# Layer 1's weight conversion: lower parts and guards offered to GpSimd, first v loads moved to SyncE, block 1 given a wider lead

## The chip, the cores and the metric

One core of one Trainium2 chip. The metric is the device time of one execution in microseconds; several runs are timed and the median counts.

## The reference

Three stages, one after the other. Linear attention on q, k, v of shape (8, 8, 576, 64) makes x of shape (4608, 512). Layer 1 takes `elu(x @ w_in) @ w_out` with 2048 hidden columns; layer 2 does the same with other weights and a rational function P(h)/Q(h) in place of elu.

```python
q_s = softmax(q, axis=-1)
k_s = softmax(k, axis=2)
kv = einsum('bhsd,bhse->bhde', k_s, v)
x = einsum('bhsd,bhde->bhse', q_s, kv)      # laid out as (4608, 512)
h = x @ moe_w_in
x = where(h > 0, h, exp(min(h, 0)) - 1) @ moe_w_out
h = x @ moe2_w_in
out = (P(h) / (Q(h) + 1e-6)) @ moe2_w_out
```

All four weight matrices arrive as 64-bit floats; q, k, v are 32-bit floats.

## The kernel before, in words

The tokens are cut into nine blocks of 512, the hidden columns into sixteen slices of 128. A tile is one layer, one block, one slice: an "in" product into one PSUM bank, the activation, and an "out" product that adds into four PSUM banks. Every operand is split into a higher part and a lower part (`copy_hi`, `sub_lo`), and each product is three matmuls: high by high, high by low, low by high. So each half of a tile is 12 matmuls of 128 by 512. The in products stand at lines 785 to 787, the out products at line 827.

Layer 1 starts while attention is still going on. The list `tiles` gives the order: block 0 with its first four slices, block 1 with its first eight, then block 0's other twelve, block 1's other eight, and after that block by block. Until then x of block 0 needs the attention of batch 0 (pairs 0 to 3, two heads each), and x of block 1 that of batch 1 (pairs 4 to 7).

A weight pair of layer 1 (`plan_w1`, line 342; eight pairs of slices, w_in and w_out, 16 loads of 1 MB) goes through these steps, each on a tile of 128 by 1024:

- SyncE loads the 64-bit words into `bits`.
- `floor` (line 321 to 323) raises the top 16 bits of each word to a lower limit, so that a tiny number cannot go wrong in the next step. It is on VectorE.
- `scale` (line 331, ScalarE) makes x from the upper 32 bits, `low` (line 327, VectorE) shifts the lower 32 bits, `join` (line 335, VectorE) puts the two together.
- `hi` (line 299, ScalarE) rounds to the higher part, and `lo` (line 302, VectorE) takes the difference.

The weights of layer 2 go through the same `plan_f32` on tiles of half that size, but `joined` is given there; for layer 1 it is None.

The order of the instructions on each engine comes from a planner in the kernel, class `Plan`. Every step is an operation with a list of engines and a cost on each. Matmuls of layers are "main" operations and get due times from 20 us on; every other operation without a rank of its own gets its due time from what follows it, less its costs and less `lead`. `run` then takes, again and again, the operation and engine that can start earliest by the planner's clock, and the lower due time where two can start at once. VectorE's cost is raised by a quarter of the time that it shares with GpSimd, GpSimd's cost is not raised. What comes out is a fixed order for each engine; on the chip each engine goes through its own list and waits where an input is late.

Three places of this plan matter here. In `plan_f32` the floor is `op(DVE(slow), floor, ...)`, and in `plan_w1` the lower part is `op(DVE(1.4), lo, ...)`. Other lower parts (the activation's, `EITHER`) go to GpSimd at 1.4 or VectorE at 0.8, whichever can start first. In `plan_pair` the four v loads of batch 0 are issued from ScalarE's queue, and the fourth is followed by a small Exp, which loads the activation table:

```python
lv = chain("load_v", ((("ACT" if first else "SP", 0.45),), b["load_v"], (), ...), take=[vkind], dma=0.83)
if n == NP - 1:
    lv["tail"] = 1.5
```

At most eight loads are under way at a time by the plan (`LANES`). Pairs of one batch are spread by `plan.lead`: 3.4 us a pair for batch 0 and 2.0 us a pair for batch 1, the first pair the earliest.

Before 100 us the planner fills gaps of TensorE with matmuls on `ident` (line 276, `keep_warm`), whose results are overwritten.

Two buffers each hold the activation's input `m` and its split output `gs`. The activation of a tile of layer 1 is ScalarE's relu (line 891) and exp (894), VectorE's elu (897), ScalarE's higher part (299), then the lower part (302) on GpSimd or VectorE; only then is `m` free again.

Of the kernel before, what the change touches and what calls it, by code (L numbers as in the profile page):

```python
# [13 lines left out]
AF = mybir.ActivationFunctionType  # L14
# [20 lines left out]
class Plan:  # L35
# [17 lines left out]
    def op(self, engines, fn, after=(), rank=0.0, take=(), free=(), extra=0.0, follow=(), dma=0.0):  # L53
        o = dict(lead=self.lead, rush=0.0, main=False, due=None, follow=[a for a in follow if a is not None], issued=None, engines=engines, fn=fn, after=[a for a in after if a is not None], rank=rank, take=take,
                 free=free, extra=extra, dma=dma, held={}, end=None, next=[], n=len(self.ops))
        waits = o["after"] + o["follow"]
        o["left"] = len(waits)
        for a in waits:
            a["next"].append(o)
        self.ops.append(o)  # L60
        return o
# [120 lines left out]
def linear_attention_elu_rational(  # L182
# [31 lines left out]
    nc = tc.nc  # L214
# [41 lines left out]
    def DVE(c=0.75):  # L256
        return (("DVE", c),)
# [4 lines left out]
    def POOL(c=1.4):  # L262
        return (("POOL", c),)
# [52 lines left out]
    def plan_f32(st_op, st_of, new_x, n, rank, x_kinds, joined=None):  # L316

        b = {}
        fast, slow = whole(n)

        def floor(e):
            top = st_of().rearrange("p n t -> p (n t)").bitcast(I16).rearrange("p (n u) -> p n u", u=4)[:, :, 3]
            nc.vector.tensor_scalar(out=top, in0=top, scalar1=FLOOR, scalar2=None, op0=ALU.max)

        def low(e):
            t = st_of()[:, :, 0]
            nc.vector.tensor_scalar(out=t, in0=t, scalar1=29, scalar2=None, op0=ALU.logical_shift_right)

        def scale(e):
            b["x"] = new_x()  # L330
            nc.scalar.activation(out=b["x"], in_=st_of()[:, :, 1].bitcast(F32), func=AF.Prelu, scale=2.0**-112, alpha=-2.0**32)

        def join(e):
            xi = b["x"].bitcast(I32)
            nc.vector.scalar_tensor_tensor(out=joined().bitcast(I32) if joined else xi, in0=xi, scalar=3, in1=st_of()[:, :, 0], op0=ALU.logical_shift_left,
                                           op1=ALU.bitwise_or)

        o1 = op(DVE(slow), floor, [st_op], rank)
        o2 = b["own"] = op(ACT(0.25 + n * 0.00095), scale, [o1], rank, take=x_kinds)
        o3 = op(DVE(fast), low, [st_op], rank)  # L340
        return op(DVE(slow), join, [o2, o3], rank), b

    def plan_w1(f, which, rank, load_rank, after):

        w = (moe_w_in, moe_w_out)[which]
        kind = f"w{f // 2}_{which}"
        b = {}

        def load(e):
            b["st"] = main.tile([P, 2 * DM, 2], I32, tag=kind, name="bits", bufs=1)  # L350
            nc.sync.dma_start(out=b["st"].rearrange("p n t -> p (n t)"), in_=w[f // 2].bitcast(I32))

        def new_x():
            (name, _), = x["own"]["held"].items()
            return at.tile([P, 2 * DM], F32, tag=name, name="x", bufs=1)

        def pairs(ap):
            return ap.rearrange("p (i n) -> p i n", i=2)

        def hi(e):  # L360
            b["hl"] = new_slots(f, which)
            copy_hi(b["hl"][:, :, 0], pairs(x["x"]))

        def lo(e):
            sub_lo(e, b["hl"][:, :, 1], pairs(x["x"]), b["hl"][:, :, 0])

        b["op"] = op(SP, load, after, load_rank, take=[kind], dma=2.6)
        o, x = plan_f32(b["op"], lambda: b["st"], new_x, 2 * DM, rank, [("x", "st")])
        own = op(ACT(1.05), hi, [o], rank)
        o = op(DVE(1.4), lo, [own], rank, free=[(("x", "st"), x["own"])])  # L370
        at_ops.append(o)
        for i in range(2):
            slot_ready[0, f + i, which], slot_owner[0, f + i, which] = o, b["op"]
        return o
# [57 lines left out]
    def pair_fns(n):  # L432
# [20 lines left out]
        def load_v(e):  # L453
            if j > 1 and b["v_op"]["held"].get("x"):
                vt = at.tile([P, 2 * TB], F32, tag="x", name="vt", bufs=1)
            elif vkind == "xs":
                vt = main.tile([P, 2 * TB], F32, tag="xs", name="vt", bufs=8)[:, 0:NS * (2 * D + 2)]
            else:
                vt = at.tile([P, NS * (2 * D + 2)], F32, tag="vb", name="vb", bufs=1)
            if j > 1:  # L460
                b["vt"] = vt[:, 0:S // D * (D + 1)].rearrange("p (j c) -> p j c", c=D + 1)
                nc.sync.dma_start(out=vt[:, 0:S // D * (D + 1)], in_=v[j, hp, :, 0:S // D * (D + 1)])
                return
            (nc.scalar if e == "ACT" else nc.sync).dma_start(out=vt, in_=v[j, hp])
            if n == NP - 1:
                nc.scalar.activation(out=spare, in_=ident[:, 0:1], func=AF.Exp)
            b["vt"] = vt.rearrange("p (j h c) -> p j h c", j=NS, h=2)

        def load_q(e):
# [188 lines left out]
    def plan_pair(j, hp, r):  # L658
        n = j * NP + hp
        b = pair_fns(n)  # L660
        kkind, vkind, qkind = b["kinds"]
        first = j == 0
        o = plan_q(n, r, None, 0.0)
        b["t_op"] = t1 = chain("q_T", (PE(0.47), b["q_T"], [o], r + 1.5), take=["bank", "qT"], free=[(qkind, b["q_op"])], extra=0.2)
        b["qc"] = chain("q_copy", (ACT(), b["q_copy"], [t1], r + 1.7), free=[("bank", t1)])

        def kT_top(e):
            b["top"] = at.tile([P, 1], F32, tag="top", name="top", bufs=2)
            nc.vector.tensor_reduce(out=b["top"], in_=flat()[:, 0:S], op=ALU.max, axis=AX.X, negate=True)

        def kT_exp(e):
            nc.scalar.activation(out=flat()[:, 0:S], in_=flat()[:, 0:S], func=AF.Exp, bias=b["top"])

        def flat():
            return b["kt"].rearrange("p j n -> p (j n)")

        def k_turn(e):
            b["tp"] = [acc_bank() if first else bank() for _ in range(2)]
            for i in range(NS):
                w = min(P, S - i * P)  # L680
                nc.tensor.transpose(b["tp"][i // 4][0:w, i % 4 * P:(i % 4 + 1) * P], flat()[:, i * P:i * P + w], ident)

        def k_back(e):
            nc.scalar.activation(out=flat()[:, 0:TB], in_=b["tp"][0], func=AF.Copy)

        def k_tail(e):
            dst, src = flat()[0:S - TB, TB:TB + P], b["tp"][1][0:S - TB, 0:P]
            if e == "ACT":
                nc.scalar.activation(out=dst, in_=src, func=AF.Copy)
            else:  # L690
                nc.vector.tensor_scalar(out=dst, in0=src, scalar1=1.0, scalar2=None, op0=ALU.mult)

        l = b["k_op"] = chain("load_k", (SP, b["load_k"], (), r - 3), take=[kkind], dma=0.82)
        lv = chain("load_v", ((("ACT" if first else "SP", 0.45),), b["load_v"], (), r - 2.2 if first else r - 2), take=[vkind],
                   dma=0.83)
        if n == NP - 1:
            lv["tail"] = 1.5
        top = chain("k_top", (DVE(0.72), kT_top, [l], r - 0.5), take=["top"])
        o = chain("k_exp", (ACT(0.7), kT_exp, [top], r - 0.4), free=[("top", top)])
        tp_kind = "acc" if first else "bank"  # L700
        kT = chain("k_turn", (PE(0.6), k_turn, [o], r - 0.3), take=[tp_kind, tp_kind, "kvd"], extra=0.2)
        o1 = chain("k_back", (ACT(), k_back, [kT], r), free=[(tp_kind, kT)])
        o2 = chain("k_tail", ((("ACT", 0.3), ("DVE", 0.25)), k_tail, [kT], r))
        kvm = chain("kv_mm", (PE(0.9), lambda e: b["kv_mm"](e, b["tp"][1]), [o1, o2, lv], r + 0.5), extra=0.2,
                    free=[(kkind, l), (vkind, lv)])
        o = chain("kv_norm", (DVE(0.33), b["kv_norm"], [kvm], r + 0.7))
        kv_ready[n] = chain("kv_div", ((("ACT", 0.31), ("DVE", 0.25)), b["kv_div"], [o], r + 0.7), free=[(tp_kind, kT)])
        kvd_of[n] = kT
        if hp % 2:
            plan_x(n, r, [state[n - 1]["qc"], b["qc"]])  # L710
# [282 lines left out]
        for which in range(2):  # L993
            w1.append(plan_w1(f, which, None, None, [w1[-6]] if len(w1) > 5 else []))
    for hp in range(NP):
        plan.lead = 0.01 + 2.0 * (NP - 1 - hp)
        plan_pair(1, hp, 0.0)
    plan.lead = 0.0
    for n, t in enumerate(tiles[:NB * KF]):
# [72 lines left out]

    with tc.manual_schedule():
        nc.vector.memset(qbias, 2.0**-48 * (1.0 + 1e-6))
        make_identity(nc, ident)

        def load_ab(e):
# [95 lines left out]
```

## Time and profile before

| what | us |
|---|---|
| median of 3 runs | 1592.34 |
| the 3 runs | 1591.29 to 1597.28 |
| the profiled execution | 1595.57 |
| span of that execution, first to last instruction | 1593.8 |
| TensorE busy with matmuls in the span | 1573.5 (99%) |
| VectorE busy | 1041.6 (65%) |
| ScalarE busy | 1040.5 (65%) |
| GpSimd busy | 762.5 (48%) |

The page names TensorE PE, VectorE DVE, ScalarE ACT, GpSimd POOL and SyncE SP. All times within the span count from its first instruction. Busy time of TensorE holds the filling matmuls on `ident`, too, and matmuls overlap in the pipeline, so it is no measure of useful work by itself. An instruction's duration holds what it waits inside its engine, for instance for access to memory; the time before it, in which the engine stood still, is listed apart as idle with what ended it.

### The profile page before, as it was taken

How to read it: one execution, taken by the hardware profiler on the slowest of the kernel's cores; microseconds unless marked ns; L12 is line 12 of the kernel's file. 1: busy time of each engine (PE TensorE's matmuls, PEld its weight loads, DVE VectorE, ACT ScalarE, POOL GpSimd, SP SyncE). 2: the span in 40 equal slices, each digit the busy share in tenths (PEclk: the TensorE clock that was granted, in tenths of full speed). 3: DMA queues.
4: the chain of work that ended last, by engine and by line, in shares of the span. 5: the costliest groups of instructions: out<-in, count | busy, mean ns of one | idle time of the engine just before them, and what ended most of it. 6: DMA issues, size and time to landing. Idle time of an engine off the chain costs nothing.

```text
span 1593.8 us, 22864 instructions
## 1 busy us (share of the span) xinstructions
PE 1573.5 (99%) x8382; PEld 1356.0 (85%) x8382; DVE 1041.6 (65%) x1627; ACT 1040.5 (65%) x1835; POOL 762.5 (48%) x551
## 2 busy tenths in 40 slices
PE   8999999999999999999999999999999999999998
PEld 7787888888888888888887888888888888888886
DVE  8888666554655556431227767686778687777776
ACT  6767655554655455444558767777777777777676
POOL 3333323232332222232657566656666666666554
PEclk9999999999999999999999999999999999999999
DMA  9513443232332322101432010101010000100000
GB/s 352 229 56 103 150 137 114 85 110 97 102 111 88 103 95 92 52 14 37 137 91 80 1 53 1 54 0 54 0 46 8 29 26 21 34 7 21 1 27 27
DMA packets 48784, 113.31 MB, mean 71 GB/s; under 512 B 5664, under 2 KB 5664, under 8 KB 46624
## 3 DMA queue, kind: packets, MB, share of 16 engines
q1 hardware_dynamic: 48096, 110.52, 20.2%
q8 instruction: 66, 1.08, 0.3%
q10 hardware_dynamic: 576, 1.33, 0.2%
q14 instruction: 46, 0.38, 0.1%
HBM read 82.47 MB, written 29.36 MB: 70 GB/s over the span
## 4 chain that ended last, share of the span: by engine, by line
PE 87%; ACT 4%; issue 4%; DVE 3%; POOL 2%; DMA 0%; POOLq 0%; DVEq 0%; ACTq 0%
PE acc L827 43%; PE ps L785 14%; PE ps L787 14%; PE ps L786 14%; POOL gs L302 2%; PE ps L639 1%; PE ps L512 1%; ACT p L930 1%; ACT s L926 1%; ACT m L936 0%; ACT m L939 0%; DVE s L942 0%; DVE m L945 0%; PE acc L276 0%; DMA e<-in_q_dram 0%
## 5 line engine op out<-in xcount | busy, mean ns | idle before, releaser
L785 PE MATMUL ps<-xs,w_in 128*128 128x512 f32 x1152 | 439.7, 382 | 6.6 <-DVE m L897 3.6
L787 PE MATMUL ps<-xs,w_in 128*128 128x512 f32 x1152 | 438.4, 381 | 0.0
L786 PE MATMUL ps<-xs,w_in 128*128 128x512 f32 x1152 | 438.4, 381 | 0.0
L827 PE MATMUL acc<-gs,w_out 128*128 128x512 f32 x1728 | 403.8, 381 | 1.3 <-POOL gs L302 0.8
L827 PEld LDWEIGHTS acc<-gs,w_out 128*128 128x128 f32 x1728 | 324.0, 189 | 52.9 <-ACT gs L299 2.8
L302 POOL TENSOR_TENSOR gs<-m,gs 128x512 fp32r<-128x512 f32 x119 | 163.0, 1370 | 360.4 <-ACT gs L299 332.0
L785 PEld LDWEIGHTS ps<-xs,w_in 128*128 128x128 f32 x1152 | 218.7, 190 | 42.1 <-issue 6.5
L786 PEld LDWEIGHTS ps<-xs,w_in 128*128 128x128 f32 x1152 | 218.7, 190 | 31.3 <-DVE xs L302 0.2
L787 PEld LDWEIGHTS ps<-xs,w_in 128*128 128x128 f32 x1152 | 218.7, 190 | 31.2
L897 DVE SCALAR_TENSOR_TENSOR m<-m,ps 128x512 f32<-128x512 f32 x144 | 98.6, 684 | 206.8 <-ACT m L894 198.1
L302 POOL TENSOR_TENSOR gs<-p,gs 128x512 fp32r<-128x512 f32 x72 | 116.3, 1615 | 235.5 <-issue 196.9
L933 POOL TENSOR_TENSOR s<-s,m 128x512 f32<-128x512 f32 x144 | 218.4, 1517 | 16.9 <-ACT m L922 16.9
L827 PE MATMUL acc<-w_out,gs 128*128 128x512 f32 x864 | 202.4, 381 | 2.6 <-ACT gs L299 1.6
L827 PE MATMUL acc<-w_out,g 128*128 128x512 f32 x864 | 199.8, 379 | 0.5 <-POOL g L302 0.5
L891 ACT ACTIVATE m<-ps 128x512 f32<-128x512 f32 x144 | 85.8, 596 | 166.9 <-PE ps L787 126.8
L942 DVE SCALAR_TENSOR_TENSOR s<-s,m 128x512 f32<-128x512 f32 x144 | 142.6, 990 | 71.7 <-ACT m L939 71.5
L827 PEld LDWEIGHTS acc<-w_out,gs 128*128 128x128 f32 x864 | 162.9, 189 | 29.4 <-POOL gs L302 4.6
L827 PEld LDWEIGHTS acc<-w_out,g 128*128 128x128 f32 x864 | 163.2, 189 | 24.0 <-POOL g L302 0.9
L930 ACT ACTIVATE p<-ps,a_sb 128x512 f32<-128x512 f32 x144 | 112.1, 779 | 80.7 <-POOL gs L302 73.9
L299 ACT ACTIVATE gs<-m 128x512 fp32r<-128x512 f32 x144 | 90.5, 629 | 92.4 <-PE acc L827 78.5
L951 DVE SCALAR_TENSOR_TENSOR p<-p,a_sb,ps 128x512 f32<-128x512 f32 x144 | 107.4, 746 | 56.9 <-ACT m L922 56.8
L955 DVE SCALAR_TENSOR_TENSOR p<-p,a_sb,m 128x512 f32<-128x512 f32 x144 | 136.6, 949 | 2.1
(124 smaller groups left out, 1906.8 us busy)
## 6 DMA issues: line engine op xcount, KB each, us to landing
x<-e SPq DMA_DIRECT2D x36, 256.0 KB, 2.0
e<-x SPq DMA_DIRECT2D x36, 256.0 KB, 3.0
out_dram<-e SPq DMA_DIRECT2D x36, 256.0 KB, 2.0
bits<-in_moe_w_in_dram SPq DMA_DIRECT2D x8, 1024.0 KB, 11.0
bits<-in_moe_w_out_dram SPq DMA_DIRECT2D x8, 1024.0 KB, 11.9
st<-in_moe_w_in_dram SPq DMA_DIRECT2D x16, 512.0 KB, 4.5
w<-st SPq DMA_DIRECT2D x32, 256.0 KB, 2.0
st<-in_moe_w_out_dram SPq DMA_DIRECT2D x16, 512.0 KB, 4.5
```

The lines of the kernel that those rows point to most:

```text
L299: nc.scalar.activation(out=hi, in_=src, func=AF.Copy)
L302: engine[e].tensor_tensor(out=lo, in0=src, in1=hi.bitcast(F32), op=ALU.subtract)
L785: nc.tensor.matmul(o, w[:, 0, kk, :], two(x[:, 0]), start=(kk == 0), stop=False)
L786: nc.tensor.matmul(o, w[:, 0, kk, :], two(x[:, 1]), start=False, stop=False)
L787: nc.tensor.matmul(o, w[:, 1, kk, :], two(x[:, 0]), start=False, stop=(kk == KD - 1))
L827: nc.tensor.matmul(turned(o), lhsT, two(rhs), start=(f == f0 and n == 0), stop=(f == f1 and n == 2))
L897: nc.vector.scalar_tensor_tensor(out=b["m"], in0=b["m"], scalar=-1.0, in1=b["h"], op0=ALU.add, op1=ALU.max)
L930: nc.scalar.activation(out=b["p"], in_=b["h"], func=AF.Identity, scale=a_sb[:, 3:4], bias=a_sb[:, 2:3])
L933: engine[e].tensor_tensor(out=b["s"], in0=b["s"], in1=b["a"], op=ALU.add)
L942: nc.vector.scalar_tensor_tensor(out=b["s"], in0=b["s"], scalar=1.0 + 1e-6, in1=b["a"], op0=ALU.add, op1=ALU.mult)
L951: nc.vector.scalar_tensor_tensor(out=b["p"], in0=b["p"], scalar=a_sb[:, 1:2], in1=b["h"], op0=ALU.add, op1=ALU.mult)
L955: nc.vector.scalar_tensor_tensor(out=b["p"], in0=b["p"], scalar=a_sb[:, 0:1], in1=b["a"], op0=ALU.add, op1=ALU.mult)
```

## The change

Five edits. The lower part of layer 1's weights goes to GpSimd at a planned 2.5 us in place of VectorE at 1.4. Layer 1's floor may go to VectorE at 1.39 or to GpSimd at 0.2 + 1024 * 0.002 = 2.25, whichever can start first. The v loads of batch 0 are issued by SyncE, with the rank of the others. The table is loaded by an Exp on `qbias` as ScalarE's first instruction. The lead of batch 1's pairs goes from 2.0 to 3.0 us a pair.

```diff
         def floor(e):
-            nc.vector.tensor_scalar(out=top, in0=top, scalar1=FLOOR, scalar2=None, op0=ALU.max)
+            engine[e].tensor_scalar(out=top, in0=top, scalar1=FLOOR, scalar2=None, op0=ALU.max)
...
-        o1 = op(DVE(slow), floor, [st_op], rank)
+        o1 = op((("DVE", slow), ("POOL", 0.2 + n * 0.002)) if joined is None else DVE(slow), floor, [st_op], rank)
...
-        o = op(DVE(1.4), lo, [own], rank, free=[(("x", "st"), x["own"])])
+        o = op(POOL(2.5), lo, [own], rank, free=[(("x", "st"), x["own"])])
...
-            (nc.scalar if e == "ACT" else nc.sync).dma_start(out=vt, in_=v[j, hp])
-            if n == NP - 1:
-                nc.scalar.activation(out=spare, in_=ident[:, 0:1], func=AF.Exp)
+            nc.sync.dma_start(out=vt, in_=v[j, hp])
...
-        lv = chain("load_v", ((("ACT" if first else "SP", 0.45),), b["load_v"], (), r - 2.2 if first else r - 2), take=[vkind],
+        lv = chain("load_v", (SP, b["load_v"], (), r - 2), take=[vkind],
                    dma=0.83)
-        if n == NP - 1:
-            lv["tail"] = 1.5
...
     for hp in range(NP):
-        plan.lead = 0.01 + 2.0 * (NP - 1 - hp)
+        plan.lead = 0.01 + 3.0 * (NP - 1 - hp)
         plan_pair(1, hp, 0.0)
...
         nc.vector.memset(qbias, 2.0**-48 * (1.0 + 1e-6))
+        nc.scalar.activation(out=spare, in_=qbias, func=AF.Exp)
         make_identity(nc, ident)
```

## Rows read from the trace of the kernel before

**Rows 1.** Windows: us, then each engine's busy us (instructions), PEclk, DMA share, GB/s.

```profile
0.00:27.30 27.30, 23.60 (x218) 19.84 (x218) 20.07 (x42) 16.78 (x29) 10.76 (x14) 1.00 0.96 375
27.30:65.00 37.70, 35.40 (x279) 28.49 (x277) 36.37 (x54) 28.32 (x49) 16.41 (x11) 1.00 0.60 219
65.00:131.00 66.00, 61.64 (x275) 52.40 (x274) 57.55 (x52) 45.99 (x56) 19.70 (x9) 0.97 0.32 125
200.00:1594.00 1394.00, 1383.89 (x7222) 1196.04 (x7220) 878.98 (x1397) 900.74 (x1595) 686.85 (x495) 1.00 0.17 56
```

**Rows 2.** Timeline of TensorE: start us, us, line, op, [idle before <- what ended it].

```profile
27.30 0.48 PE L785 MATMUL ps<-xs,w_in 128*128 128x512 f32 x1
...
34.68 3.74 PE L276 MATMUL acc<-ident 128*128 128x128 f32 x32
...
39.39 1.78 PE L827 MATMUL acc<-gs,w_out 128*128 128x512 f32 x7 [0.54 <-DVE w_out L302]
...
51.44 0.95 PE L520 MATMUL ps<-vb,kt 128*64 128x65 f32 x20 [1.62 <-ACT kt L689]
```

**Rows 3.** Waits of TensorE: waited for, us in total, times, longest us.

```profile
PE ps L785 <- DVE m L897: 3.6, 2, 2.2
```

**Rows 4.** Chain of work that ended last: start us, us, what; two of its pieces.

```profile
0.73 3.77 DMA e<-in_q_dram
...
25.95 1.04 DVE w_in L302
```

**Rows 5.** Timeline of VectorE, ScalarE and GpSimd, 16 to 40 us, on the first weights.

```profile
16.32 1.27 DVE L323 TENSOR_SCALAR bits<-bits 128x1024 int16<-128x1024 int16 x1
...
23.89 1.06 ACT L299 ACTIVATE w_in<-x 128x1024 fp32r<-128x1024 f32 x1 [0.29 <-DVE x L335]
...
30.30 2.19 DVE L323 TENSOR_SCALAR bits<-bits 128x1024 int16<-128x1024 int16 x1
...
33.84 1.04 ACT L299 ACTIVATE w_out<-x 128x1024 fp32r<-128x1024 f32 x1
...
38.12 1.21 DVE L302 TENSOR_TENSOR w_out<-x,w_out 128x1024 fp32r<-128x1024 f32 x1
```

**Rows 6.** DMA issues: line's tiles, queue, count, KB each, us to landing.

```profile
e<-x SPq DMA_DIRECT2D x36, 256.0 KB, 3.0
```

**Rows 7.** Timeline of VectorE and GpSimd where both work, 95 to 120 us.

```profile
95.94 1.28 POOL L302 TENSOR_TENSOR gs<-m,gs 128x512 fp32r<-128x512 f32 x1 [1.89 <-ACT gs L299]
...
96.05 2.56 DVE L335 SCALAR_TENSOR_TENSOR x<-x,bits 128x1024 int32<-128x1024 int32 x1
...
112.91 3.05 DVE L335 SCALAR_TENSOR_TENSOR x<-x,bits 128x1024 int32<-128x1024 int32 x2
...
113.19 4.98 POOL L302 TENSOR_TENSOR gs<-m,gs 128x512 fp32r<-128x512 f32 x1 [3.56 <-ACT gs L299]
...
115.80 1.40 DVE L323 TENSOR_SCALAR bits<-bits 128x1024 int16<-128x1024 int16 x1
```

**Rows 8.** Instructions on tile bits, 0 to 60 us: duration ns min/median/max, first and last start.

```profile
L327 DVE TENSOR_SCALAR bits<-bits x5: 695/999/1585, 20.4 to 56.0; 128x1024 int32<-128x1024 int32 x5
L335 DVE SCALAR_TENSOR_TENSOR x<-x,bits x5: 1232/1521/2029, 21.9 to 58.4; 128x1024 int32<-128x1024 int32 x5
```

**Rows 9.** Groups of VectorE and GpSimd, 65 to 131 us: count | busy us, mean ns | idle before.

```profile
L335 DVE SCALAR_TENSOR_TENSOR x<-x,bits 128x1024 int32<-128x1024 int32 x10 | 15.9, 1601 | 1.1 <-ACT x L331 0.7
L323 DVE TENSOR_SCALAR bits<-bits 128x1024 int16<-128x1024 int16 x9 | 13.3, 1473 | 0.0
L327 DVE TENSOR_SCALAR bits<-bits 128x1024 int32<-128x1024 int32 x9 | 9.1, 1023 | 0.0
L302 DVE TENSOR_TENSOR w_in<-x,w_in 128x1024 fp32r<-128x1024 f32 x6 | 8.4, 1398 | 0.4 <-ACT w_in L299 0.2
L302 DVE TENSOR_TENSOR w_out<-x,w_out 128x1024 fp32r<-128x1024 f32 x5 | 7.2, 1442 | 0.2 <-ACT w_out L299 0.2
...
L302 POOL TENSOR_TENSOR gs<-m,gs 128x512 fp32r<-128x512 f32 x9 | 19.7, 2189 | 42.1 <-ACT gs L299 42.1
```

## The prediction

> **What bounds the kernel now.** I read the windows by stage first. From 200 us on TensorE is busy 1383.89 of 1394 us [rows 1]; nothing that the change touches acts there, since layer 1's weights are ready by then. So the change is worth what is lost before. In the first 27.3 us TensorE does no product of a layer: the first one starts at 27.30 [rows 2]. Between 27.3 and 65 us it is busy 35.40 of 37.70 us, but the busy time holds a filler of 3.74 us [rows 1, 2]. Between 65 and 131 us it stands still 4.4 us, and its granted clock falls to 0.97 on the mean, that is, part of the stretch ran at the lower of its two levels, 1.2 GHz, after these pauses; 3% of 66 us is 2.0 us [rows 1].
>
> The windows also say who is the limit in these stages: VectorE is busy 36.37 of 37.70 us and then 57.55 of 66 us, GpSimd only 16.41 and 19.70 [rows 1]. The chain of waits runs through VectorE from the first q load to the lower part of the first w_in [rows 4]. So far this speaks for moving work to GpSimd.
>
> The timeline of both engines speaks against it. A join on VectorE, which takes 1.23 us at best, took 2.56 us when it began 0.11 us behind a lower part on GpSimd of 1.28 us: it waited for that one to end [rows 7, 8]. The other way round, a lower part on GpSimd took 4.98 us because two joins and a floor followed one another on VectorE from 112.91 to 117.20 us; it ended at 118.17 [rows 7]. Operations with SBUF inputs on these two engines exclude each other here. Of such work the kernel gets no more done by sharing it out.
>
> **The change part by part.** The sum is made against the profiled execution, 1595.57 us, span 1593.8. That one lies 3.2 us above the median of 1592.34; I take the same difference off the median. A measurement of this kernel can tell about 0.5% from no change, 8 us, so the bounds are 1584.4 and 1600.3.
>
> *Term 1, the start.* The first q load lands 3.77 us after its issue [rows 4]; a load of the same 256 KB alone takes 3.0 [rows 6]. Before, four v loads run beside it from ScalarE's queue; in SyncE's queue they come behind the first q and k. So 0.8 us. The v loads are 4 x 128 x 650 x 4 bytes = 1.33 MB, at the 375 GB/s of this stretch 3.5 us [rows 1], but they stood ahead of the weights before as well, so the weights' loads land no later. Their issues now pass through SyncE ahead of the later q, k and weight loads, and these leave ScalarE; I cost that at nothing, as the DMA share is 0.96 [rows 1] and the transfers cover the issue; without that cover it would be four issues. The table load at once costs nothing either: ScalarE has 16.78 us of work in 27.3 [rows 1], and before the first Exp it waits for data. The floor at 16.32 stood on VectorE for 1.27 us ahead of attention work [rows 5]; on GpSimd it is off that queue, -1.27. The lower part of w_in is not seen on GpSimd at this size: the nearest row is 1.28 us for half the size [rows 7], so 2.56. The high part ends at 24.95 (23.89 + 1.06), so on GpSimd the lower part would end at 27.5, where VectorE ended at 27.0 (25.95 + 1.04) [rows 4, 5]: +0.5. Sum -0.8 - 1.27 + 0.5 = -1.6. Bounds: +0.5 if nothing upstream moves; -0.8 - 2 x 1.27 - 1.21 = -4.5 if all that VectorE is rid of by then counts.
>
> *Term 2, the gap at 35 us.* TensorE fills 3.74 us and then stands 0.54 until VectorE has made the lower part of w_out [rows 2]. Its high part was done at 34.88; VectorE came to it at 38.12, 3.2 us later, and took 1.21 [rows 5]. On GpSimd one other lower part may stand in front (1.4), and it takes 1.35 more. Of the floor at 30.30, 2.19 us [rows 5], I count half as gained upstream, because on GpSimd it holds up VectorE's joins in turn. -3.2 + 1.4 + 1.35 - 1.1 = -1.5. Bounds +1.35 and -4.3 (the whole gap).
>
> The price of a floor on GpSimd is not in the trace. Below: 1.27, as on VectorE; above: 2.56, two inputs of that size. I take 2.1, nearer the upper row because that is GpSimd's own.
> The Trainium skill (GPSIMD Engine Reference, 3.1 Elementwise) gives 1.03 cycles an element for an operation with one input; at its 1.2 GHz I estimate 0.9 us, by which a floor there would be cheaper than on VectorE and term 4 below about 0. No run so far shows it.
>
> *Term 3, block 1's pairs.* The wider lead puts the first pair of batch 1 due 9 us ahead in place of 6, the next 6 in place of 4. The wait of 1.62 us at 51.44 on such a pair's key tail [rows 2] should shrink: -1.0; bounds -1.6, and +2.0 if the pairs now displace the first weights on ScalarE and VectorE by about two operations.
>
> *Term 4, the weights from 65 to 131 us.* At their undisturbed prices the operations that exclude one another need 10 x 1.23 (joins) + 9 x 1.27 (floors) + 9 x 0.70 (lows) + 11 x 1.21 (lower parts) + 9 x 1.28 (activation's lower parts on GpSimd) = 54.8 of 66 us [rows 5, 7, 8, 9]. Eleven lower parts at 2.56 add 14.9, so 69.7: 3.7 us too much; with nine floors at 2.1 on GpSimd another 7.5. Some of it is relieved since the activation's lower parts go to VectorE when GpSimd is taken, and some can slip past 131 us, because the last slices are used last. VectorE's long runs, which held GpSimd for 4.98 us, get rarer: of the 3.6 us waited for VectorE's m [rows 3] I take 2 back, and put 3 of new waiting against it: +1. Bounds -5.6 (3.6 and the 2.0 of the clock) and +15 (14.9 with no relief).
>
> Sum: -1.6 - 1.5 - 1.0 + 1.0 = -3.1. 1592.3 - 3.1 = **1589.2 us**.
>
> **The rivals.** *GpSimd becomes the wait (slower).* Lower parts of 2.56 us, stretched by whatever VectorE holds, stand in GpSimd's queue in front of the activation's; ScalarE's relu then waits for `m`, of which there are two, and behind it in ScalarE's queue the scale and high part of the next weights; TensorE runs out of products. It decides from where the excess of term 4 can no longer slip: then about 14 of the 3.7 + 7.5 us and of the same in 27 to 65 us fall on TensorE, and with terms 1 to 3 at -3 it is +11: 1603. For it: the 4.98 us row [rows 7] and a planner that does not raise GpSimd's cost. Against: GpSimd's idle time, 46 of 66 us [rows 1].
> The Trainium skill says the same as a rule (SBUF — State Buffer, Who interferes with whom): the pair of ports is an exclusive lock, taken by VectorE with two SBUF inputs and by GpSimd for a whole instruction. By that rule the trace agrees for joins and lower parts; for the floor, with one input, the rule asks for a two-port mode, and the row of 2.19 us says that it waits too. The page Perfetto Trace Analysis (Optimizing Scalar/DVE Operations) adds that moving work between these two might not help.
>
> *VectorE alone was the limit (much faster).* GpSimd's holes take the work without collisions: terms at their lower bounds, -4.5 - 4.3 - 1.6 - 5.6 = -16; two thirds of that, -11: 1581. For it: VectorE's 96% and 87%. Against: 54.8 of 66 us are already exclusive work.
>
> *It doesn't do what it says.* The planner has GpSimd free at the wrong moments and leaves floors on VectorE, the start is set by the loads as before, and term 4 eats the little: 1592.
>
> **How the numbers follow.** Forecast (a few us faster) 0.35, slower 0.25, much faster 0.22, nothing 0.18. Of the slower case two thirds lie above 1600.3, of the much faster nearly all below 1584.4, and some of the forecast's spread beyond either. So faster 0.24, same 0.57, slower 0.19. The range, 1580 to 1602, takes in the forecast, the middle of the much faster case and most of the slower one; the bounds of term 4 set its upper end.
>
> **What would show it.** First product at 25.7 rather than 27.30; filler and wait before the first out products under 3 us; lower parts of the weights on GpSimd at 2.6 us where alone and up to 5 beside joins; VectorE's busy share in 27 to 131 us down by some 30 us; waits of TensorE in 65 to 131 us between 3 and 6 us, on GpSimd's lower parts instead of VectorE's m. The forecast is wrong if these waits pass 12 us, or if the first product starts before 23.5 us and the later waits vanish.

## The result, and the profile after

The changed kernel takes 1615.98 us at the median (five runs, 1614.2 to 1619.99), the kernel before 1592.34 beside it. The ratio is 1.015 with a 95% interval of 1.0135 to 1.0164: slower by 23.6 us, where 3.1 us faster was forecast, and outside the range of 1580 to 1602. The profiled execution has a span of 1614.2 us, 20.4 more than before.

The windows of the changed kernel, in the columns of [rows 1]:

```profile
0.00:27.30 27.30, 22.18 (x223) 18.64 (x225) 19.79 (x40) 17.56 (x33) 18.97 (x18) 1.00 0.96 362
27.30:65.00 37.70, 29.75 (x197) 23.26 (x197) 26.94 (x39) 23.49 (x36) 36.36 (x16) 0.91 0.63 242
65.00:131.00 66.00, 51.08 (x224) 41.09 (x217) 52.64 (x43) 35.48 (x50) 60.61 (x17) 0.91 0.24 96
131.00:200.00 69.00, 66.95 (x341) 57.32 (x344) 35.60 (x54) 41.79 (x75) 33.11 (x21) 0.99 0.30 98
200.00:1614.00 1414.00, 1404.26 (x7383) 1213.68 (x7372) 901.48 (x1433) 919.50 (x1644) 695.67 (x502) 1.00 0.17 57
```

The window of the kernel before that [rows 1] leaves out:

```profile
131.00:200.00 69.00, 69.00 (x397) 59.26 (x396) 48.60 (x87) 48.67 (x108) 28.73 (x22) 1.00 0.37 126
```

All of the loss lies where the change acts. From 200 us on TensorE stands still 9.7 us, as before (10.1). Between 27.3 and 131 us it stands 7.95 + 14.92 = 22.9 us; before it was 2.3 + 4.4 = 6.7 [rows 1]. The granted clock is 0.91 in both stretches; 9% of 103.7 us is 9.3 us, against 2.0 before. Together that is 23.5 us more. The filler in this stretch fell from 3.7 us [rows 2] to 1.3, so 2.5 us of the standing have only changed their name, and 2.1 us come after 131 us: 23.1. The span grew by 20.4; this sum is higher in part because it counts the low clock also while TensorE stands. Counted in matmuls, the traces have 576 of the layers' products by 200 us, and 676 before: 100 at 0.22 us each are 22 us.

The third column of busy times has VectorE down from 36.37 to 26.94 and from 57.55 to 52.64. The last one, GpSimd, is up from 16.41 to 36.36 of 37.70 and from 19.70 to 60.61 of 66 us. The limit has moved to GpSimd, which hardly rests. The groups of GpSimd from 27.3 to 131 us say with what (count, then busy us, mean ns and idle time before):

```profile
L323 POOL TENSOR_SCALAR bits<-bits 128x1024 int16<-128x1024 int16 x10 | 52.9, 5352 | 0.0
L302 POOL TENSOR_TENSOR w_in<-x,w_in 128x1024 fp32r<-128x1024 f32 x7 | 18.5, 2637 | 0.1
L302 POOL TENSOR_TENSOR w_out<-x,w_out 128x1024 fp32r<-128x1024 f32 x5 | 15.7, 3140 | 3.5 <-ACT w_out L299 3.5
```

Ten floors take 52.9 us, more than the twelve lower parts beside them (34.2). The view of line 323 (duration in ns: least, median, largest; first and last start) shows that this isn't a matter of collisions alone:

```profile
L323 POOL TENSOR_SCALAR bits<-bits x12: 4312/5352/6228, 16.8 to 115.6; 128x1024 int16<-128x1024 int16 x12
```

The shortest floor on GpSimd takes 4.31 us. The plan has 2.25, and the prediction bounded it by 2.56.

How this reaches TensorE is seen at the first weights, in the timeline of the changed kernel:

```profile
25.88 1.06 ACT L299 ACTIVATE w_in<-x 128x1024 fp32r<-128x1024 f32 x1 [0.89 <-DVE x L335]
...
28.29 4.74 POOL L323 TENSOR_SCALAR bits<-bits 128x1024 int16<-128x1024 int16 x1
...
32.86 2.35 POOL L302 TENSOR_TENSOR w_in<-x,w_in 128x1024 fp32r<-128x1024 f32 x1
...
35.26 0.80 PE L783 MATMUL ps<-xs,w_in 128*128 128x512 f32 x1 [4.68 <-POOL w_in L302]
```

The high part of the first w_in is ready at 26.94. Its lower part on GpSimd begins at 32.86, since the plan had put the floor of a later weight ahead of it, in the belief that it would be over in 2.25 us. TensorE waits 4.68 us for it, and then its clock is at half: in the chain of waits the matmuls that follow stand 0.43 us apart until 40.29, and 0.22 from there.

```profile
36.05 0.43 PE ps L781
...
40.29 0.22 PE ps L782
```

The waits of TensorE between 27 and 131 us (in total, times, longest):

```profile
PE acc L823 <- DVE gs L302: 6.6, 3, 4.5
PE ps L783 <- POOL w_in L302: 4.7, 1, 4.7
PE ps L782 <- DVE xs L302: 4.2, 1, 4.2
PE acc L823 <- ACT gs L299: 4.0, 2, 3.5
PE acc L823 <- POOL gs L302: 2.2, 1, 2.2
```

Most of them name another engine than GpSimd. The rows behind three of the longest show why. For the 3.5 us, ScalarE's higher part came late because in ScalarE's own list a scale stood in front of it, and that waited for a floor.

```profile
115.64 6.23 POOL L323 TENSOR_SCALAR bits<-bits 128x1024 int16<-128x1024 int16 x1
...
121.90 1.13 ACT L331 ACTIVATE x<-bits 128x1024 f32<-128x1024 f32 x1 [7.38 <-POOL bits L323]
...
122.94 0.61 ACT L299 ACTIVATE gs<-m 128x512 fp32r<-128x512 f32 x1
...
123.61 0.48 PE L823 MATMUL acc<-gs,w_out 128*128 128x512 f32 x1 [3.52 <-ACT gs L299]
```

For the 4.5 us, the activation's lower part came late because in VectorE's list a floor and a low stood in front of it, and these took 3.47 and 2.81 us beside two lower parts on GpSimd (the first began at 100.37); the least of each before is 1.27 and 0.70.

```profile
101.27 3.47 DVE L323 TENSOR_SCALAR bits<-bits 128x1024 int16<-128x1024 int16 x1
...
103.50 3.28 POOL L302 TENSOR_TENSOR w_in<-x,w_in 128x1024 fp32r<-128x1024 f32 x1
...
104.52 2.81 DVE L327 TENSOR_SCALAR bits<-bits 128x1024 int32<-128x1024 int32 x1
...
107.25 0.68 DVE L302 TENSOR_TENSOR gs<-m,gs 128x512 fp32r<-128x512 f32 x1
...
107.98 4.33 PE L823 MATMUL acc<-gs,w_out 128*128 128x512 f32 x11 [4.54 <-DVE gs L302]
```

The 4.2 us have the same form with the floors of GpSimd beside: x's lower part on VectorE stood behind a floor of 3.67 us there. So the floors hurt through the lists that wait for them, and floors and lower parts both hurt through stretched operations on VectorE.

### The profile page after: what moved, and what is told of

Its sections match the earlier page's. It is cut to its first block, busy times and chain, and to the rows that moved or that the text cites. A ratio compares the mean times of both kernels' runs of the same rounds, so it can differ in the third digit from the quotient of the medians.

```text
span 1614.2 us, 22798 instructions
## 1 busy us (share of the span) xinstructions
PE 1574.2 (98%) x8342; PEld 1354.0 (84%) x8342; DVE 1036.4 (64%) x1606; ACT 1037.8 (64%) x1836; POOL 844.7 (52%) x571
## 4 chain that ended last, share of the span: by engine, by line
PE 85%; ACT 4%; POOL 4%; DVE 3%; issue 2%; DMA 1%; POOLq 0%; SPq 0%; DVEq 0%; ACTq 0%
PE acc L823 42%; PE ps L781 14%; PE ps L783 14%; PE ps L782 14%; POOL gs L302 1%; POOL bits L323 1%; PE ps L637 1%; PE ps L510 1%; DVE bits L327 1%; ACT p L926 1%; POOL w_in L302 1%; POOL w_out L302 1%; ACT s L922 1%; ACT m L932 0%; DMA st<-in_moe_w_in_dram 0%
## 5 line engine op out<-in xcount | busy, mean ns | idle before, releaser
L823 PE MATMUL acc<-gs,w_out 128*128 128x512 f32 x1728 | 408.8, 384 | 14.9 <-DVE gs L302 6.6
L302 POOL TENSOR_TENSOR gs<-m,gs 128x512 fp32r<-128x512 f32 x110 | 144.4, 1313 | 311.3 <-ACT gs L299 294.9
L299 ACT ACTIVATE gs<-m 128x512 fp32r<-128x512 f32 x144 | 90.3, 627 | 92.6 <-PE acc L823 77.2
```

The source lines that it names most:

```text
L299: nc.scalar.activation(out=hi, in_=src, func=AF.Copy)
L302: engine[e].tensor_tensor(out=lo, in0=src, in1=hi.bitcast(F32), op=ALU.subtract)
L823: nc.tensor.matmul(turned(o), lhsT, two(rhs), start=(f == f0 and n == 0), stop=(f == f1 and n == 2))
```

## The experiments

The theory after the result: floors cost 4.3 us and more on GpSimd, and the lists of all engines wait for them. The rivals: the lower parts and the access that the two engines share; or the loads and the lead. The kernel before ran beside each group of runs at 1593.9 us (1593.84 to 1593.95), and the ratios are to it.

### One part undone, or one part alone

Floors back on VectorE, all else as changed:

```diff
-            engine[e].tensor_scalar(out=top, in0=top, scalar1=FLOOR, scalar2=None, op0=ALU.max)
+            nc.vector.tensor_scalar(out=top, in0=top, scalar1=FLOOR, scalar2=None, op0=ALU.max)
...
-        o1 = op((("DVE", slow), ("POOL", 0.2 + n * 0.002)) if joined is None else DVE(slow), floor, [st_op], rank)
+        o1 = op(DVE(slow), floor, [st_op], rank)
```

> The changed kernel with all floors of layer 1 back on VectorE, all else of the change kept. Theory (the floors' price: 4.31 us on GpSimd where nothing disturbs them, planned at 2.25, twelve of them): most of the 23.6 us go, 1588 to 1596. Rival (the lower parts on GpSimd and the shared access): at most a third goes, 1606 to 1614. Rival (loads and lead): nothing goes, 1612 to 1618.

Measured: 1600.9 us, 1.0044 (1.0027 to 1.006). About 15 us go, which is most of it and more than either rival allowed. But the theory's window ended at 1596, and the time stays 7 us above the kernel before: something else costs as well.

The kernel before with the floors offered and nothing else:

```diff
-            nc.vector.tensor_scalar(out=top, in0=top, scalar1=FLOOR, scalar2=None, op0=ALU.max)
+            engine[e].tensor_scalar(out=top, in0=top, scalar1=FLOOR, scalar2=None, op0=ALU.max)
...
-        o1 = op(DVE(slow), floor, [st_op], rank)
+        o1 = op((("DVE", slow), ("POOL", 0.2 + n * 0.002)) if joined is None else DVE(slow), floor, [st_op], rank)
```

> The kernel before with only the floors offered to GpSimd at the planned 2.25 us. Theory (the floors' price): slower than before by 10 to 25 us, 1602 to 1617, with GpSimd's floors at 4.3 us or more. Rival (the lower parts): within 4 us of before. Rival (loads and lead): within 4 us of before.

Measured: 1613.16 us, 1.0118 (1.0102 to 1.0135), +19.3 us, as the theory had it. All 16 floors go to GpSimd here, at 4.27 us or more:

```profile
L323 POOL TENSOR_SCALAR bits<-bits x16: 4272/4790/5952, 13.9 to 120.0; 128x1024 int16<-128x1024 int16 x16
```

The kernel before with the lower parts on GpSimd and nothing else:

```diff
-        o = op(DVE(1.4), lo, [own], rank, free=[(("x", "st"), x["own"])])
+        o = op(POOL(2.5), lo, [own], rank, free=[(("x", "st"), x["own"])])
```

> The kernel before with only the lower parts of layer 1's weights on GpSimd at the planned 2.5 us. Theory (the floors' price): within 5 us of before, 1588 to 1597, since the lower parts take 2.36 us undisturbed, less than planned. Rival (the lower parts and the shared access): 10 to 20 us slower, 1602 to 1612. Rival (loads and lead): as before.

Measured: 1601.77 us, 1.005 (1.0035 to 1.0065), +7.9 us. The theory had 1597 at most, so it falls short; the rival had 10 us at least, so it is right in kind and too high. The groups of both engines from 65 to 131 us, which answer to [rows 9], show where it comes from:

```profile
L335 DVE SCALAR_TENSOR_TENSOR x<-x,bits 128x1024 int32<-128x1024 int32 x11 | 20.2, 1858 | 1.3 <-ACT x L331 1.3
L327 DVE TENSOR_SCALAR bits<-bits 128x1024 int32<-128x1024 int32 x9 | 18.2, 2024 | 0.0
L323 DVE TENSOR_SCALAR bits<-bits 128x1024 int16<-128x1024 int16 x9 | 17.1, 1899 | 0.0
...
L302 POOL TENSOR_TENSOR w_in<-x,w_in 128x1024 fp32r<-128x1024 f32 x6 | 19.4, 3236 | 0.0
L302 POOL TENSOR_TENSOR w_out<-x,w_out 128x1024 fp32r<-128x1024 f32 x4 | 13.1, 3278 | 4.0 <-ACT w_out L299 4.0
```

The low on VectorE takes 2024 ns on the mean, 1023 before; the floor 1899, 1473 before; the join 1858, 1601 before [rows 9]. VectorE is rid of eleven lower parts (8.4 + 7.2 us), and yet it is busy longer in this stretch, 61.12 us beside 57.55. A join and two of the activation's lower parts are new in it (some 3 us); the rest of what it gave up, 15.6 us, comes back as longer lows, floors and joins. The Trainium skill (Perfetto Trace Analysis, Optimizing Scalar/DVE Operations) says that moving work between these two engines might not help; this run agrees with that sentence.

Loads, table and lead as changed, nothing moved to GpSimd (the edits of the change's diff at `load_v`, `lv`, the Exp on `qbias` and):

```diff
-        plan.lead = 0.01 + 2.0 * (NP - 1 - hp)
+        plan.lead = 0.01 + 3.0 * (NP - 1 - hp)
```

> The kernel before with only the v loads on SyncE, the table at once and the lead of 3.0: no work moved to GpSimd. Theory (the floors' price) and the rival of the lower parts: within 4 us of before, by the prediction's terms 1 and 3 some 1 to 2 us faster, 1588 to 1593. Rival (loads and lead): 10 us slower or more.

Measured: 1592.86 us, 0.9994 (0.9984 to 1.0004), no difference that can be told. The three parts alone give +19.3, +7.9 and -1.0, in sum 26.2; the whole change has 23.6. They nearly add up.

The changed kernel with the lower parts back on VectorE:

```diff
-        o = op(POOL(2.5), lo, [own], rank, free=[(("x", "st"), x["own"])])
+        o = op(DVE(1.4), lo, [own], rank, free=[(("x", "st"), x["own"])])
```

> The changed kernel with the lower parts back on VectorE, floors still offered to GpSimd. If floors and lower parts add up (18 to 19 us and 7 to 8 us alone, loads and lead -1): 1608 to 1613. If lower parts hurt only because floors fill GpSimd, they cost more together than alone: 1602 to 1607.

Measured: 1610.11 us, 1.0104 (1.0088 to 1.012): they add up here, too. This run has the plainest picture of a list held up. Between a query's exponential and its product with the reciprocal sum, the plan of GpSimd has three floors:

```profile
36.58 14.13 POOL L323 TENSOR_SCALAR bits<-bits 128x1024 int16<-128x1024 int16 x3
...
50.54 1.04 POOL L575 TENSOR_TENSOR qt<-qt,mx 128x512 f32<-128x512 f32 x1
...
51.64 1.11 PE L581 MATMUL ps<-ident,qt 128*128 128x128 f32 x4 [7.24 <-POOL qt L575]
```

At the planned price three floors are 6.75 us; they took 14.13, and TensorE stood still for 7.24 us.

### The wrong price, or the work itself

The changed kernel with the floor's price in the plan near the measured one:

```diff
-        o1 = op((("DVE", slow), ("POOL", 0.2 + n * 0.002)) if joined is None else DVE(slow), floor, [st_op], rank)
+        o1 = op((("DVE", slow), ("POOL", 0.2 + n * 0.0041)) if joined is None else DVE(slow), floor, [st_op], rank)
```

> The changed kernel with the planner's price of a floor on GpSimd at 0.2 + 1024 * 0.0041 = 4.4 us in place of 2.25; the plan then has 8 of the 16 floors on GpSimd in place of 12. If the harm was the planner's wrong price (the lists of all engines made for a GpSimd that is twice as fast), the time comes near that without floors there, 1600.9: 1599 to 1605. If the harm is the work itself, at 4.3 us and more each, two thirds of the 15 us stay: 1608 to 1613.

Measured: 1611.24 us, 1.0113 (1.0095 to 1.0131), as the second expectation had it. Knowing the price saves 5 us of 15; the rest stays with the eight floors that the plan still gives to GpSimd. It does so because, by its code, it compares when an operation can begin, not when it ends: an idle GpSimd wins over a VectorE that is free 1 us later and three times as fast.

The floors alone offered at the planned price, but on GpSimd as a 32-bit maximum, which leaves the guard out there (the plan's line as in the run with the floors alone):

```diff
...
+            if e == "POOL":
+                top = st_of()[:, :, 1].bitcast(F32)
+                nc.gpsimd.tensor_scalar(out=top, in0=top, scalar1=-3e38, scalar2=None, op0=ALU.max)
+                return
...
```

> The kernel before with floors offered to GpSimd, but on GpSimd the floor is a maximum of the 32-bit upper halves as floats with -3e38, at the same stride of 8 bytes and count of 1024: it leaves the guard out there. If 16-bit access is what makes 4.3 us: 1.1 to 2.4 us each, and a time of 1588 to 1600. If it is the single-input loop of GpSimd or the stride: still 4 us or more and a time as with the 16-bit floors alone, 1609 to 1616.

Measured: 1603.09 us, 1.0059 (1.0043 to 1.0075). The view of that line:

```profile
L325 POOL TENSOR_SCALAR bits<-bits x16: 2925/3829/4937, 13.8 to 109.1; 128x1024 f32<-128x1024 f32 x16
```

At least 2.93 us in place of 4.27: at the same stride and count the 16-bit integer form costs 1.35 us more than the 32-bit float one, and neither expectation is met. Since the planned price is the same, this kernel and the one with the floors alone have the same order on every engine. The sixteen floors take 59.5 us in place of 77.2, 17.7 less, and the time falls by 10.1 us: the length by itself costs, at more than half a microsecond of the kernel for each on GpSimd. What makes the other 2.9 us, the stride of 8 bytes or the operation with one input, was not tried apart.

### Can the lower parts be planned better?

Lower parts on GpSimd, floors on VectorE, loads and lead as changed, and the plan counts the shared time in full on both engines (cut to the plan's lines):

```diff
...
-                cost += SHARED * min(cost, max(0.0, self.free_at.get("POOL", 0.0) - t))
+                cost += min(cost, max(0.0, self.free_at.get("POOL", 0.0) - t))
+            if e == "POOL" and t < UNTIL:
+                cost += min(cost, max(0.0, self.free_at.get("DVE", 0.0) - t))
...
```

> Lower parts on GpSimd, floors on VectorE, loads and lead as changed, but the planner adds the whole overlap of VectorE and GpSimd to the cost of the later one (a quarter, and on VectorE's side alone, before). If the 7 us of the lower parts come from waits that the plan does not foresee: 1590 to 1596. If the shared access has no room for lower parts of 2.4 us: 1598 to 1606, as without this.

Measured: 1597.87 us, 1.0023 (1.0014 to 1.0033), between the two. Its windows from 27.3 us on:

```profile
27.30:65.00 37.70, 34.00 (x256) 26.89 (x256) 32.72 (x45) 26.75 (x45) 22.47 (x14) 1.00 0.57 210
65.00:131.00 66.00, 66.00 (x334) 56.94 (x329) 54.57 (x45) 47.44 (x62) 43.72 (x18) 1.00 0.36 137
131.00:200.00 69.00, 64.99 (x359) 54.05 (x358) 51.93 (x95) 45.91 (x97) 33.78 (x23) 0.95 0.37 120
```

From 65 to 131 us TensorE doesn't stand at all, at full clock, with the lower parts on GpSimd. What is lost now lies on both sides of this stretch. The first product of a layer comes at 33.12, and by 65 us the trace has 84 of the layers' products, 97 before. From 131 to 200 us TensorE stands 4.0 us and its clock is 0.95, where before it didn't stand and had its full clock. So I split off the start: lower parts on GpSimd for slices 4 to 15 only, the planner as it was,

```diff
...
-        o = op(POOL(2.5), lo, [own], rank, free=[(("x", "st"), x["own"])])
+        o = op(POOL(2.5) if f >= 4 else DVE(1.4), lo, [own], rank, free=[(("x", "st"), x["own"])])
```

> Loads and lead as changed, floors on VectorE, lower parts on GpSimd only for slices 4 to 15 (12 of 16), planner as it was. If the 7 us of the lower parts arise in the stretch from 65 us on, as its waits say: 1597 to 1602, as with all 16. If they arise at the start: 1590 to 1594.

Measured: 1600.8 us, 1.0038 (1.0025 to 1.005), as with all 16. Up to 65 us this trace is that of the loads and the lead without lower parts (from 27.3 us TensorE is busy 34.54 us beside 34.67); from there on it falls behind. So the cost of the lower parts arises from 65 us on. And the same with the shared time in full from 60 us of the plan:

```diff
...
+                cost += (SHARED if t < 60.0 else 1.0) * min(cost, max(0.0, self.free_at.get("POOL", 0.0) - t))
+            if e == "POOL" and 60.0 <= t < UNTIL:
+                cost += min(cost, max(0.0, self.free_at.get("DVE", 0.0) - t))
...
```

> As e14_late, and from 60 us of the plan on the planner counts the whole overlap of VectorE and GpSimd as cost. If the lower parts hurt by waits that the plan does not foresee, the stretch from 65 to 131 us loses its pauses as in e11_excl, without that one's later start: 1587 to 1592, below both kernels. If the shared access has no room for them: 1597 to 1602.

Measured: 1593.68 us, 0.9997 (0.9988 to 1.0006), above the first expectation's window by 2 us. The two windows from 65 to 131 us, without and with the new counting:

```profile
65.00:131.00 66.00, 60.10 (x259) 50.48 (x258) 58.69 (x43) 43.58 (x54) 48.17 (x17) 0.95 0.27 110
```

```profile
65.00:131.00 66.00, 63.88 (x294) 54.94 (x294) 50.07 (x39) 43.87 (x57) 47.01 (x18) 1.00 0.37 143
```

TensorE stands 3.8 us less, 3.3 us of clock come back, and the 7 us are gone. GpSimd is as busy in both (48 and 47 us). VectorE's fall from 58.69 to 50.07 us is no shorter waiting inside its operations: it has four operations on the weights fewer in this stretch, which now come after 131 us, and over all sixteen tiles its floors, lows and joins take 73.4 us, 74.2 without the new counting. What has changed is whether TensorE waits for what stands behind a collision. Without the new counting TensorE waits twice for VectorE's elu, 4.8 us in all, each time because a join in front of it was held by a lower part on GpSimd; here is the longer one:

```profile
121.56 3.30 POOL L302 TENSOR_TENSOR w_out<-x,w_out 128x1024 fp32r<-128x1024 f32 x1
...
122.60 3.35 DVE L335 SCALAR_TENSOR_TENSOR x<-x,bits 128x1024 int32<-128x1024 int32 x1
...
125.88 0.68 DVE L893 SCALAR_TENSOR_TENSOR m<-m,ps 128x512 f32<-128x512 f32 x1
...
126.61 0.48 PE L781 MATMUL ps<-xs,w_in 128*128 128x512 f32 x1 [2.80 <-DVE m L893]
```

With the new counting TensorE waits for the elu no more. So the 7 us came from collisions that the plan didn't foresee: they still happen, but TensorE no longer waits for what stands behind them. Even so the kernel before isn't beaten, nor is the one with loads and lead alone (1592.86): moving the lower parts is then worth nothing.

### The loads and the lead, each alone

The kernel before with the loads and the table alone:

```diff
-            (nc.scalar if e == "ACT" else nc.sync).dma_start(out=vt, in_=v[j, hp])
-            if n == NP - 1:
-                nc.scalar.activation(out=spare, in_=ident[:, 0:1], func=AF.Exp)
+            nc.sync.dma_start(out=vt, in_=v[j, hp])
...
-        lv = chain("load_v", ((("ACT" if first else "SP", 0.45),), b["load_v"], (), r - 2.2 if first else r - 2), take=[vkind],
+        lv = chain("load_v", (SP, b["load_v"], (), r - 2), take=[vkind],
...
+        nc.scalar.activation(out=spare, in_=qbias, func=AF.Exp)
```

> The kernel before with only the v loads on SyncE and the table at once. If loads in order of need bring the start forward (term 1 of the prediction, 0.8 us): 1592 to 1594, beside 1593.9 of before. If they delay the later k and the first weights (the third w load landed 2 us later in the changed kernel), the start is later: 1594 to 1598.

Measured: 1592.89 us, 0.9989 (0.998 to 0.9998), 1 to 2 us faster, by the loads and the table at once.

The kernel before with the lead alone:

```diff
-        plan.lead = 0.01 + 2.0 * (NP - 1 - hp)
+        plan.lead = 0.01 + 3.0 * (NP - 1 - hp)
```

> The kernel before with only the lead of batch 1's pairs at 3.0 us. If the wait at 51 us was what the lead removes (term 3): 1591 to 1593.5. If earlier pairs only displace the first weights: 1594 to 1598.

Measured: 1593.06 us, 0.9992 (0.9983 to 1.0001): not told from no change.

No version is shown to beat the kernel before by more than 0.2%; the best ratio is that of the v loads and the table alone.

## Why the prediction was wrong

**The price of a floor on GpSimd** is the step that failed. It read "Below: 1.27, as on VectorE; above: 2.56, two inputs of that size. I take 2.1". The upper bound was a row of another operation (32-bit, two inputs, no gaps) scaled to the size, and was taken as an end because one input seemed less than two. Measured: 4.27 us at least (the floors alone) and 5.35 at the median of the changed kernel. The page GPSIMD Engine Reference (3.1 Elementwise) of the Trainium skill led to an estimate of 0.9 us by its figure for one input; the trace does not agree, by a factor of nearly five. Alone the floors cost 19.3 us, against "7.5" of exclusive time in term 4, from which +1 was left. Twelve floors at the plan's price are 27 us, in the trace 61.5. No run has floors of 2.1 us on GpSimd, so what the change would do at the price that was forecast stays open; at 2.93 us and more they still cost 9.2 us alone.

**The rival "GpSimd becomes the wait"** had the right engine and the right end: ScalarE's list held up, TensorE out of products. It had a chance of 0.25, and its price was 1603. Its path was another one. It had ScalarE's relu wait for `m`; from 27.3 to 131 us that wait for lower parts fell, from 7.6 to 5.0 us. What grew is the wait of ScalarE's scale, for floors and for lower parts that still read the x that it writes:

```profile
ACT x L331 <- POOL w_in L302: 10.6, 3, 5.5
ACT x L331 <- POOL bits L323: 10.6, 3, 7.4
```

And it named the lower parts, where the floors cost more. That 1603 lies near the 1601.8 of the lower parts alone says little, since it had the floors in it.

**Term 4** was set at +1 with a bound of +15. The lower parts alone cost 7.9 us, within the bound and far from the choice. The sum of exclusive work was the wrong ground even so. It took floors on GpSimd as excluding VectorE's joins, as term 2 did, and they don't (last section). And with a plan that counts the collisions nine of the lower parts fit into the 66 us, with TensorE not standing at all; the rest slips past 131 us, as the term allowed.

**Term 1**: the first q load was to land 0.8 us earlier. VectorE's first reduction began at 3.54 in place of 4.53:

```profile
3.54 0.69 DVE L537 TENSOR_REDUCE mx<-e 128x8 f32<-128x512 f32 x1 [2.69 <-DMA e<-in_q_dram]
...
7.32 0.69 DVE L537 TENSOR_REDUCE mx<-e 128x8 f32<-128x512 f32 x1 [2.25 <-DMA e<-in_q_dram]
```

So that part was right, and VectorE comes to the k behind it sooner as well (4.32; 6.05 before), but the next row shows VectorE idle for 2.25 us until the second q. Of the 0.8 us plus what else could move, 1.1 us came out in the median of the run with loads and table alone. The rest of the term, -1.27 for the floor and +0.5 for the lower part, was not gained: the first product came at 29.90, not 25.7, and the one with the lower part of w_in at 35.26, behind the floor. The floor is not all of it, since with loads, table and lead alone the first product came at 28.80. With the lower parts alone, the lower part of the first w_in ended at 27.48, as forecast (27.5), and yet the first product came at 29.23: it waited for VectorE, which was late with the lower part of the layer's input x.

```profile
25.11 2.37 POOL L302 TENSOR_TENSOR w_in<-x,w_in 128x1024 fp32r<-128x1024 f32 x1
...
29.23 0.48 PE L785 MATMUL ps<-xs,w_in 128*128 128x512 f32 x1 [0.72 <-DVE xs L302]
```

The first product's time decides little by itself: with the lead alone it came at 30.27, and the time was not longer.

**Term 2** foresaw a gap 1.5 us shorter through a lower part on GpSimd. In the run with the lower parts alone, the lower part of the first w_out did end sooner, at 37.11 (39.33 before), but TensorE still filled 3.45 us in this stretch (3.74 before) and the first out product began at 38.85 (38.17 before): no gain, since the fillers stand in TensorE's list ahead of the product. **Term 3**, -1.0 for the lead, is met by number (-0.9), but the runs can't tell it from zero (0.9983 to 1.0001).

The rival that VectorE alone was the limit fell with the first windows: VectorE was busy 14 us less, and the time rose. The sign that I had named came: waits past 12 us between 65 and 131 us; they are 14.9.

## What to carry to other kernels

Before work goes to another engine, take its price there from the same operation with the same type and stride, or measure it alone; a row of a different operation is no bound. In a list made by a planner an operation that is twice as long as planned is paid by every engine whose list waits for it, and a planner that picks by earliest start will keep choosing the slow engine even when it knows the price. Where VectorE and GpSimd share access to SBUF, look at how far the durations spread, not only at which of the two is idle, and let the plan count the overlap on both, so that nothing urgent stands behind a collision.

## What was not expected of the hardware

A floor on GpSimd doesn't hold up operations with two inputs on VectorE. In the changed kernel a join of 1.22 us, which is as short as undisturbed, ran within the floor from 36.16 to 40.47; in the run with the lower parts back on VectorE a join of 1.17 us and two lower parts of 1.22 us ran within the three floors that begin at 36.58. A tiny operation with one input, 0.15 us otherwise, took 2.30 us and ended with the floor at 21.1:

```profile
16.79 4.33 POOL L323 TENSOR_SCALAR bits<-bits 128x1024 int16<-128x1024 int16 x1
...
18.85 2.30 DVE L571 TENSOR_SCALAR mx<-mx 128x8 f32<-128x8 f32 x1
...
36.16 4.31 POOL L323 TENSOR_SCALAR bits<-bits 128x1024 int16<-128x1024 int16 x1
...
37.53 1.22 DVE L335 SCALAR_TENSOR_TENSOR x<-x,bits 128x1024 int32<-128x1024 int32 x1
```

With lower parts (two inputs) on GpSimd it is otherwise: there the join waited [rows 7]. The page SBUF — State Buffer (Who interferes with whom) of the Trainium skill lets two SBUF inputs on VectorE exclude any GpSimd operation that reads SBUF; for these floors the trace does not agree. Why the two kinds of operation on GpSimd differ was not tried.
